# Transposing w3 by DMA instead of on TensorE, with its loads complete, a later start of the output product, and loads that wait for DMA transposes beside the first batch

## Chip, cores and metric

One core of a Trainium2 chip. The metric is the device time of one execution in microseconds (us). The engines carry the profile's names: PE is TensorE, PEld its weight loads, DVE VectorE, ACT ScalarE, POOL GpSimd, SP SyncE; a q behind a name (SPq, POOLq) marks a DMA that this engine issued. PSUM is the memory in which PE leaves its results, and from which ACT and DVE fetch them. Ratios in this document are the mean time of one kernel's runs over that of the other's runs of the same rounds, so they are not quite the ratio of the medians quoted beside them.

## The reference, cut to what matters

```python
# q, k, v: (4, 5824, 256); w1, w2: (256, 1024); w3: (1024, 1024); w_out: (1024, 256)
qn = q / (norm(q, axis=1) + 1e-6);  kn = k / (norm(k, axis=1) + 1e-6)
a = softmax(kn.transpose(0, 2, 1) @ qn / tau)     # 256 x 256 for each batch
x = (v @ a).reshape(4 * 5824, 256)
out = ((x @ w1) * (x @ w2)) @ w3 @ w_out
```

The kernel folds the small matrix of each batch into w1 and w2 ("folds", giving `Wf`), so a and b come directly from transposed v. It also multiplies w3 by w_out once (`W_sb`), so that the output product has 256 columns. For that product w3 must be transposed, and how this is done is what changes.

## The kernel before: the parts that matter

All work of one batch is issued in pairs: `emit_ab` computes 128 rows of a and of b for up to 512 tokens (a chunk), ACT casts a, DVE multiplies by b. Finished pairs are kept in `pend`; once `W_sb` is ready, `emit_out` multiplies them by it. Everything else hangs on an agenda: `at(t, cost, fn)` runs `fn` when the kernel's own clock (units of about a microsecond of TensorE work, zero at the start of a batch) reaches `t`.

```python
def pe_transpose(dst, src, tag, on_act):
    m = psum.tile([P, 8, P], BF16, tag=tag, ..., bufs={"ab": 4, "out": 3}[tag])
    for i, blk in enumerate(src):
        nc.tensor.transpose(m[:, i, :], blk, ident_b)
    if on_act: nc.scalar.copy(dst, m)
    else:      nc.vector.tensor_copy(dst, m)
...
def gate():                      # POOL waits for a recent product before it issues a load
    if last_ab[0] is not None:
        nc.gpsimd.tensor_copy(gate_t, last_ab[0][:1, :1])
...
for h in range(2):               # w3 in two halves, then w_out, then v's third piece
    js = slice(h * FT // 2, (h + 1) * FT // 2)
    nc.gpsimd.dma_start(out=w3_bf[:, js, :], in_=w3r[:, js, :])
nc.gpsimd.dma_start(out=wout_sb, ...)
load_piece("v", 0, 2)
...
def w3_transpose(jt):
    pe_transpose(w3T[jt // 2][:, jt % 2, :, :],
                 [w3_bf[:, jt, lt * P : (lt + 1) * P] for lt in range(FT)], "ab", jt % 2 == 0)

def w_unit(jt):                  # one of eight w products: W_sb[:, jt] = w3T . w_out
    m = psum.tile([P, 512], F32, tag="ab", ..., bufs=4)
    ...
# agenda of batch 0
for jt in range(FT):
    at((12.0 if jt < 4 else 15.0) + jt, 0.5, lambda jt=jt: w3_transpose(jt))
    at(24.0 + jt, 0.87, lambda jt=jt: w_unit(jt))
at(14.0, 0.0, lambda: transpose_piece(0, 2))       # v's third piece, by DMA
```

The a and b tiles, the w products, the folds and the transposes of w3 share four PSUM buffers (tag `ab`), used in turn.

## Time and profile before

| | before |
|---|---|
| time, median of the first three runs | 580.99 us (580.4 to 581.26) |
| span in the profile | 578.5 us |
| TensorE (PE) busy | 98% |
| VectorE (DVE), ScalarE (ACT) busy | 65%, 59% |
| PE transposes of w3 | 64, in 8 groups, from 52.99 us |

The prediction below shows the lines that carry this.

### The profile page before, as it was taken

The numbers are of one execution on the slowest core, as the hardware profiler recorded it, in microseconds if no ns is written. First come the engines' busy times: TensorE is split into PE (matmuls) and PEld (weight loads), VectorE is DVE, ScalarE is ACT, GpSimd is POOL, SyncE is SP. The second block draws the span as 40 slices with busy tenths as digits, with TensorE's granted clock in tenths as the row PEclk, the third lists the DMA queues.
The fourth block names the chain that finished last, engine by engine and source line by source line (L and its number), as shares of the span: only waits on it lengthen the run. The fifth ranks groups of instructions, "written<-read, shape, count | busy, mean of one in ns | idle before, by whom it ended". The sixth has DMA issues, their size and how long they took to land.

```text
span 578.5 us, 10224 instructions
## 1 busy us (share of the span) xinstructions
PE 565.4 (98%) x3826; PEld 360.8 (62%) x3834; DVE 376.8 (65%) x601; ACT 341.4 (59%) x628; POOL 64.1 (11%) x142
## 2 busy tenths in 40 slices
PE   8799999999999999999999999999999999999996
PEld 4665676766656566666666666666665656656664
DVE  0047545888877567788766667778876656565564
ACT  0046535777765576777765476767765554454453
POOL 5240021110000202001000112001100000000000
PEclk9999999999999999999999999999999999999999
DMA  8999989773543798555652699754563325311011
GB/s 164 211 206 199 172 152 208 162 167 78 120 100 109 132 233 167 111 113 122 129 126 74 147 199 177 166 110 87 146 133 87 83 77 146 83 41 71 37 73 56
DMA packets 66113, 74.85 MB, mean 129 GB/s; under 512 B 45840, under 2 KB 49808, under 8 KB 66064
## 3 DMA queue, kind: packets, MB, share of 16 engines
q0 software_dynamic: 15376, 39.46, 39.7%
q1 hardware_dynamic: 50544, 34.61, 20.0%
q8 instruction: 30, 0.49, 0.3%
q14 instruction: 19, 0.16, 0.1%
q10 hardware_dynamic: 144, 0.13, 0.1%
HBM read 78.91 MB, written 23.86 MB: 178 GB/s over the span
## 4 chain that ended last, share of the span: by engine, by line
PE 89%; DMA 6%; DVE 1%; ACT 1%; issue 1%; POOL 0%; ACTq 0%; POOLq 0%
PE o L452 27%; PE a L419 27%; PE b L419 26%; PE G L188 5%; DMA q<-in_q_dram 4%; PE fold L344 2%; PE w L570 1%; DMA v<-in_v_dram 1%; ACT as L425 1%; DVE abs L428 1%; POOL k L109 0%; DVE osb L473 0%; PE row L272 0%; PE ss L283 0%; ACT e L307 0%
## 5 line engine op out<-in xcount | busy, mean ns | idle before, releaser
L428 DVE TENSOR_TENSOR abs<-as,b 128x512 bf16<-128x512 bf16 x352 | 240.9, 687 | 147.5 <-ACT as L425 136.5
L425 ACT CAST as<-a 128x512 bf16<-128x512 f32 (+1 forms) x384 | 215.4, 562 | 172.6 <-DVE abs L428 83.7
L452 PE MATMUL o<-W_sb,abs 128*128 128x256 bf16 x1440 | 218.2, 273 | 0.5 <-ACT osb L472 0.4
L419 PEld LDWEIGHTS <-Wf 128*128 128x128 bf16 x1536 | 148.9, 98 | 98.2 <-issue 1.7
L419 PE MATMUL a<-vT,Wf 128*128 128x512 bf16 x704 | 209.6, 379 | 0.4
L419 PE MATMUL b<-vT,Wf 128*128 128x512 bf16 x704 | 209.5, 379 | 0.1
L452 PEld LDWEIGHTS <-abs 128*128 128x128 bf16 x1440 | 140.6, 98 | 86.3 <-issue 0.6
L197 DVE TENSOR_TENSOR acc<-acc,sq 128x1024 f32<-128x1024 f32 x66 | 80.4, 1218 | 0.1
L411 POOL COPY gate_t<-abs 1x1 bf16<-1x1 bf16 x39 | 10.3, 265 | 394.7 <-DVE abs L428 386.6
L188 PE MATMUL G<-k,q 128*128 128x256 bf16 x276 | 49.8, 273 | 0.0
L185 ACT ACTIVATE sq<-q 128x512 f32<-128x512 bf16 x66 | 41.8, 633 | 0.0
L185 ACT ACTIVATE sq<-k 128x512 f32<-128x512 bf16 x66 | 41.6, 630 | 0.0
L473 DVE COPY osb<-o 128x512 f32<-128x512 f32 x44 | 30.1, 685 | 0.4 <-PE o L452 0.4
L188 PEld LDWEIGHTS <-q 128*128 128x128 bf16 x276 | 27.0, 98 | 3.1
L472 ACT COPY osb<-o 128x512 f32<-128x512 f32 x44 | 25.7, 585 | 3.8 <-PE o L452 1.7
L274 ACT ACTIVATE kr<-row 128x256 f32<-128x256 f32 x4 | 1.5, 384 | 31.0 <-PE row L272 31.0
L109 POOL DMA_DIRECT2D q<-in_q_dram x28 | 15.0, 537 | 14.3 <-DMA k<-in_k_dram 5.7
L351 ACT ACTIVATE Wf<-fold,rs 128x512 bf16<-128x512 f32 x16 | 10.8, 687 | 8.9 <-PE fold L344 4.7
L344 PE MATMUL fold<-w,e 128*128 128x512 bf16 x61 | 16.0, 379 | 0.1
L109 POOL DMA_DIRECT2D v<-in_v_dram x25 | 13.5, 540 | 6.6 <-issue 4.9
L109 POOL DMA_DIRECT2D k<-in_k_dram x25 | 13.8, 550 | 3.4 <-DMA k<-in_k_dram 1.9
L353 DVE TENSOR_SCALAR Wf<-fold,rs 128x512 bf16<-128x512 f32 x16 | 11.8, 748 | 2.1 <-PE fold L344 1.8
(103 smaller groups left out, 197.3 us busy)
## 6 DMA issues: line engine op xcount, KB each, us to landing
out_dram<-osb SPq DMA_DIRECT2D x44, 512.0 KB, 3.0
k<-in_k_dram POOLq DMA_DIRECT2D x19, 512.0 KB, 8.9
v<-in_v_dram POOLq DMA_DIRECT2D x19, 512.0 KB, 5.2
q<-in_q_dram POOLq DMA_DIRECT2D x18, 512.0 KB, 5.9
w_wout<-in_moe_w_dram POOLq DMA_DIRECT2D x2, 1024.0 KB, 16.2
k<-in_k_dram POOLq DMA_DIRECT2D x4, 320.0 KB, 6.8
v<-in_v_dram POOLq DMA_DIRECT2D x4, 320.0 KB, 4.9
q<-in_q_dram POOLq DMA_DIRECT2D x4, 256.0 KB, 10.5
```

What stands on the lines that cost most here:

```text
L109: nc.gpsimd.dma_start(out=pieces[nm, n, pi][:, lo:hi, :], in_=qk_main[nm, n][0][:, pi * PIECE + lo : pi * PIECE + hi, :])
L185: nc.scalar.activation(out=dst[:, :, part, :], in_=src[:, o : o + 2, :], func=AF.Square)
L188: nc.tensor.matmul(G[:, ct, :], lhsT=qt[:, i, ct * P : (ct + 1) * P], rhs=kt[:, i, :], start=(pr == 0 and part == 0 and ct == 0), stop=(pr ...
L197: nc.vector.tensor_add(accs[n], accs[n], sqs[0])
L344: nc.tensor.matmul(st["fold", i], lhsT=st["e"][:, c2, c1 * P : (c1 + 1) * P], rhs=w12[:, c2, w, h * 512 : (h + 1) * 512], start=(c2 == 0), ...
L353: nc.vector.tensor_scalar_mul(dst, st["fold", i], st["rs"][:, c1 : c1 + 1])
L419: nc.tensor.matmul(t[:, :n], lhsT=Wf[b][:, ct, w, j * P : (j + 1) * P], rhs=rhs_of(b, c, ct), start=(ct == 0), stop=(ct == CT - 1),)
L425: nc.scalar.copy(a_sb[:, :n], tiles[0][:, :n])
L428: nc.vector.tensor_mul(ab, a_sb, tiles[1])
L452: nc.tensor.matmul(tl[s // 2][:, s % 2, :], lhsT=lhsT, rhs=W_sb[:, j, :], start=(j == 0 and s % 2 == 0), stop=(j == FT - 1 and (s % 2 == 1 ...
L472: nc.scalar.copy(o[:, 0:2, :], tl[0])
L473: nc.vector.tensor_copy(o[:, 2:4, :], tl[1])
```

## The change

The intent: take the transposes off PE, where time is scarce, and give them to the DMA queues. For that w3 is loaded whole, as the last of the early loads; four DMA transposes follow; the w products, and with them the output product, begin a little later; so more pairs must be kept, and the first 16 lie in free tiles of q. In batch 0 the first load after a DMA transpose of v waits ("hold") until that transpose has landed.

```diff
+    def hold(src):
+        nc.gpsimd.tensor_copy(gate_t, src)
...
+        if b == 0 and c < 2:
+            if j % 4 == 0:
+                held[0] = in_pool.tile([P, 4, 512], BF16, tag="q", ...)
+            ab = held[0][:, j % 4, :]
+        else:
+            ab = work.tile([P, 512], BF16, tag="ab_sb", ...)
...
+    def transpose_w3():
+        for h in range(FT // 2):
+            m = in_pool.tile([P, 2, FT, P], BF16, tag="k", ...)
+            nc.sync.dma_start_transpose(m, w3_bf[:, 2 * h : 2 * h + 2, :])
+            w3T.append(m)
...
-    for h in range(2):
-        js = slice(h * FT // 2, (h + 1) * FT // 2)
-        nc.gpsimd.dma_start(out=w3_bf[:, js, :], in_=w3r[:, js, :])
+    load_piece("v", 0, 2)
     nc.gpsimd.dma_start(out=wout_sb, ...)
-    load_piece("v", 0, 2)
+    nc.gpsimd.dma_start(out=w3_bf, in_=w3r)
...
+            at(15.0, 0.0, transpose_w3)
+            at(15.0, 0.0, lambda: transpose_piece(0, 2))
             for jt in range(FT):
-                at((12.0 if jt < 4 else 15.0) + jt, 0.5, lambda jt=jt: w3_transpose(jt))
-                at(24.0 + jt, 0.87, lambda jt=jt: w_unit(jt))
-            at(14.0, 0.0, lambda: transpose_piece(0, 2))
+                at(26.0 + 1.2 * jt, 0.87, lambda jt=jt: w_unit(jt))
# ... the loads of batch 0 get later times; scores of batch 1 (its products of k and q) from 58 (before 52) to 120 ...
+            if before is not None and b == 0:
+                at(t, 0.0, lambda w=before: hold(...))      # an element of the transposed v
```

More of the change, by code (lines that the diff above doesn't have):

```diff
@@ L406 @@
     last_ab = [None]
+    held = [None]
     def gate():
@@ L425, in emit_ab @@
         nc.scalar.copy(a_sb[:, :n], tiles[0][:, :n])
-        ab = work.tile([P, 512], BF16, tag="ab_sb", name=f"abs_{b}_{c}_{j}", bufs=8 * NDEF + 6)
+        if b == 0 and c < 2:
+            if j % 4 == 0:
+                held[0] = in_pool.tile([P, 4, 512], BF16, tag="q", name=f"abq_{c}_{j}", bufs=IN_BUFS["q"])
+            ab = held[0][:, j % 4, :]
+        else:
+            ab = work.tile([P, 512], BF16, tag="ab_sb", name=f"abs_{b}_{c}_{j}", bufs=8 * NDEF + 6)
         if n == 4 * P:
@@ L492 @@
     wout_sb = w3_wout[:, FT * F : FT * (F + D)].rearrange("p (l d) -> p l d", d=D)
-    w3T = {}
-    def new_w3T():
-        m = wf_pool.tile([P, 2, 2, FT, P], BF16, tag="Wf", name="w3T_wf")
-        for h in range(2):
-            w3T[h] = work.tile([P, 2, FT, P], BF16, tag="sq", name=f"w3T_{h}", bufs=2)
-            w3T[2 + h] = m[:, h]
+    w3T = []
+    def transpose_w3():
+        for h in range(FT // 2):
+            m = in_pool.tile([P, 2, FT, P], BF16, tag="k", name=f"w3T_{h}", bufs=IN_BUFS["k"])
+            nc.sync.dma_start_transpose(m, w3_bf[:, 2 * h : 2 * h + 2, :])
+            w3T.append(m)
     w3r = moe_w3.rearrange("(jh jl) l -> jl jh l", jl=P)
@@ L533 @@
     load_piece("v", 0, 1)
-    for h in range(2):
-        js = slice(h * FT // 2, (h + 1) * FT // 2)
-        nc.gpsimd.dma_start(out=w3_bf[:, js, :], in_=w3r[:, js, :])
+    load_piece("v", 0, 2)
     nc.gpsimd.dma_start(out=wout_sb, in_=moe_w_out.rearrange("(lh ll) c -> ll lh c", ll=P))
-    load_piece("v", 0, 2)
+    nc.gpsimd.dma_start(out=w3_bf, in_=w3r)
     squares("k", 4, whole)
@@ L556 @@
     soft0[4]()
-    new_w3T()
-    def w3_transpose(jt):
-        pe_transpose(
-            w3T[jt // 2][:, jt % 2, :, :], [w3_bf[:, jt, lt * P : (lt + 1) * P] for lt in range(FT)],
-            "ab", jt % 2 == 0,
-        )
     w_ready = [False]
@@ L591, in make_agenda @@
             at(8.0, 0.5, lambda: transpose_half_on_pe(0, 1, 1, False))
+            at(15.0, 0.0, transpose_w3)
+            at(15.0, 0.0, lambda: transpose_piece(0, 2))
             for jt in range(FT):
-                at((12.0 if jt < 4 else 15.0) + jt, 0.5, lambda jt=jt: w3_transpose(jt))
-                at(24.0 + jt, 0.87, lambda jt=jt: w_unit(jt))
-            at(14.0, 0.0, lambda: transpose_piece(0, 2))
-            loads = [("v", 0, 3, 14.0), ("v", 0, 4, 34.0), ("v", 0, 5, 54.0)]
-            loads += [("qk", 1, pi, t) for pi, t in enumerate([22.0, 30.0, 40.0, 52.0, 66.0, 80.0])]
@@ L598, in make_agenda @@
-            loads += [("v", 1, pi, t) for pi, t in enumerate([96.0, 108.0, 122.0])]
-            t0, t1 = 52.0, 120.0
-        else:
-            loads = [("v", b, pi, t) for pi, t in [(3, 1.0), (4, 20.0), (5, 34.0)]]
+                at(26.0 + 1.2 * jt, 0.87, lambda jt=jt: w_unit(jt))
+            moves = [("v", 0, 3, 29.0), ("qk", 1, 0, 38.0), ("qk", 1, 1, 43.0), ("v", 0, 4, 50.0), ("qk", 1, 2, 58.0)]
+            moves += [("qk", 1, 3, 63.0), ("v", 0, 5, 70.0), ("qk", 1, 4, 81.0), ("qk", 1, 5, 87.0)]
@@ L602, in make_agenda @@
+            moves += [("v", 1, 0, 96.0), ("v", 1, 1, 106.0), ("v", 1, 2, 116.0)]
+            t0, t1 = 58.0, 120.0
+        else:
+            moves = [("v", b, 3, 1.0), ("qk", n, 0, 4.0), ("qk", n, 1, 12.0), ("v", b, 4, 20.0), ("qk", n, 2, 27.0)]
+            moves += [("v", b, 5, 34.0), ("qk", n, 3, 44.0), ("qk", n, 4, 58.0), ("qk", n, 5, 72.0)]
+            moves += [("v", n, 0, 84.0), ("v", n, 1, 96.0), ("v", n, 2, 108.0)]
+            moves = [m for m in moves if m[1] < B]
             t0, t1 = 16.0, 104.0
-            if n < B:
-                loads += [("qk", n, pi, t) for pi, t in enumerate([4.0, 12.0, 27.0, 44.0, 58.0, 72.0])]
-                loads += [("v", n, pi, t) for pi, t in enumerate([84.0, 96.0, 108.0])]
@@ L606, in make_agenda @@
-        for nm, m, pi, t in loads:
+        before = (0, 2) if b == 0 else None
+        for nm, m, pi, t in moves:
+            if before is not None and b == 0:
+                at(t, 0.0, lambda w=before: hold(vTs[w[0]][1][:1, 0, :1] if w[1] == NP_ - 1 else vTs[w[0]][0][:1, w[1] * PIECE, 0, :1]))
+            at(t, 0.0, gate)
             if nm == "qk":
-                at(t, 0.0, gate)
                 at(t, 0.0, lambda m=m, pi=pi: load_qk(m, pi))
+                before = None
             else:
-                at(t, 0.0, gate)
@@ L612, in make_agenda @@
                 at(t, 0.0, lambda m=m, pi=pi: load_piece("v", m, pi))
-                at(t + 8.0, 0.0, lambda m=m, pi=pi: transpose_piece(m, pi))
+                at(t + (4.0 if b == 0 else 8.0), 0.0, lambda m=m, pi=pi: transpose_piece(m, pi))
+                before = (m, pi)
         if n == B:
```

## The prediction

> **What bounds the kernel now.** I read the page's busy shares first, then the chain of work that ended last, then the timeline of the stretch that the change touches (50 to 80 us), then where the batches meet (172 to 188 us), and last the DMA landings by stretch.
>
> ```profile
> PE 565.4 (98%) x3826; PEld 360.8 (62%) x3834; DVE 376.8 (65%) x601; ACT 341.4 (59%) x628; POOL 64.1 (11%) x142
> PE 89%; DMA 6%; DVE 1%; ACT 1%; issue 1%; POOL 0%; ACTq 0%; POOLq 0%
> ```
>
> PE is the bound: 98% busy, and 89% of the chain is PE. The 6% of DMA in the chain is the start (loads until about 37 us), which the change leaves alone: the same loads come in the same order up to the second piece of v. So time can only be won by taking work or idle gaps off PE, and can only be lost by new gaps on it. As "busy" is no proof of full speed, I also counted columns: matmuls in each 10 us, at 2.4 columns per ns, fill 9.4 to 10.9 us of each stretch from 40 us to 570 us. The only holes are 60 to 70 us (0.56 us) and the batch changes (about 0.5 us at 170, 300 and 440 us). A hidden reserve of ten microseconds does not exist.
>
> What the change touches is this, from the timeline of 28 to 80 us (columns: start, length, engine, line, operation, and in brackets the idle time before and who ended it):
>
> ```profile
> 52.12 0.59 PE L419 MATMUL a<-vT,Wf 128*128 128x512 bf16 x2
> 52.55 0.59 PE L419 MATMUL b<-vT,Wf 128*128 128x512 bf16 x2
> 52.99 0.61 PE L132 MATMUL tr_I-703_704<-ident_b,w_wout 128*128 128x128 bf16 x8
> 53.43 0.60 PE L419 MATMUL a<-vT,Wf 128*128 128x512 bf16 x2
> 53.63 1.01 ACT L134 COPY w3T<-tr_I-703_704 128x1024 bf16<-128x1024 bf16 x1 [0.29 <-PE tr_I-703_704 L132]
> ...
> 55.77 0.68 DVE L136 COPY w3T<-tr_I-724_725 128x1024 bf16<-128x1024 bf16 x1
> ...
> 56.51 0.43 PEld L132 LDWEIGHTS <-w_wout 128*128 128x128 bf16 x7 [0.29 <-issue]
> ...
> 62.46 0.43 PEld L132 LDWEIGHTS <-w_wout 128*128 128x128 bf16 x7 [0.41 <-issue]
> ...
> 65.38 1.03 PE L570 MATMUL w<-w_wout,w3T 128*128 128x256 bf16 x8
> 65.38 0.75 PEld L570 LDWEIGHTS <-w3T 128*128 128x128 bf16 x7 [0.41 <-issue]
> ```
>
> The reader is to see three things. A group of eight transposes starts at 52.99 and the next matmul starts at 53.43, so it takes 0.44 us of PE, 55 ns each, although one is listed with 219 ns (latency). Each group is copied out of PSUM by ACT (1.01 us) or DVE (0.68 us), between the casts and products of the a/b pairs. And in three places the weight load sat idle 0.29 to 0.41 us, called "issue": the next transpose or product waited for a PSUM buffer that such a copy still held.
>
> **What the Trainium skill says.** "TensorE: Matmul & The Clock Gate", section "Part 4: PE-mode transpose", gives about 275 ns for a 128x128 transpose in one kernel's context, with a copy out of PSUM after it. The trace agrees on the copy; as a cost in a pipelined group it measures 55 ns, and I use that: with 275 ns the gain would look like 17.6 us, which is wrong here. "Advanced Engine Details and Errata", section "X-Bar Transpose (TRN2)", says that transpose DMAs are as fast as regular ones. The trace agrees only where nothing else moves (512 KB):
>
> ```profile
> vT<-v SPq DMA_TRANSPOSE x1, 3.6
> ...
> vT<-v SPq DMA_TRANSPOSE x1, 9.3
> ```
>
> The first is from 150 to 162 us, the second from 80 to 100 us with q, k and v loads beside it; the last number is us from issue to landing. "DMA: Bandwidth & Descriptors", section "Rules for kernel authors", says that a transpose next to ordinary DMAs needs nothing. So the new waits are not for correctness; they keep transposes from being stretched.
>
> **The change part by part.**
> Removed from PE: 64 transposes of w3, 8 groups x 0.445 us = 3.56 us. Waits around them: from 52.99 to 65.38 us are 12.39 us, in which nine a/b pairs run. A pair is 0.86 us (52.12 to 52.99 less rounding), so 7.74 us; the remaining 4.65 us are transposes (3.56) and about 1.1 us of gaps. From 40.42 (first pair) to 52.99 the same count leaves no gap, and from 65.38 to the first output product at 75.60 none either. So the whole stretch offers 4.6 us.
> Removed from ACT and DVE: 4 x 1.01 and 4 x 0.68 us. Worth nothing beyond those gaps, as neither bounds this stretch (at 0.58 and 0.69 us per pair against PE's 0.86).
> Added: four DMA transposes of w3, 512 KB each, on SP's queue, ahead of the transpose of v's third piece. They start when w3 is in. In the kernel before the last of the early loads was v's third piece, and the first DMA transpose, which waits for it, starts at 58.54:
>
> ```profile
> 58.54 6.61 SPq L155 DMA_TRANSPOSE vT<-v  x2
> ```
>
> Now w3 is last, the bytes are the same, so I take 58.5 for w3. With the loads held back, each takes 3.6 to 3.9 us to land; wholly one after the other they land at 62.4, 66.3, 70.2, 74.1 and v's piece at 78.0; overlapped, with an issue of about 1.6 us each, by about 70.
> Needed: the changed order on PE puts the first w product after 28 pairs, two folds and three groups of v transposes: 40.42 + 28 x 0.86 + 2 x 0.43 + 3 x 0.445 = 66.7 us; then w1 at 68.4, w2 and w3 at 70.2, w4 and w5 at 72.8, w6 and w7 at 75.4, and chunk 4, the first that reads v's third piece, at 77.1. Each tile serves two w products (needed 66.7, 70.2, 72.8, 75.4). Even the serial landing meets all four and misses chunk 4 by 0.9 us; the overlapped one has 4 us or more to spare. I choose no stall.
> Moved: the output product begins about 1.5 us later (37.3 us of PE work after the first pair, before 33.8), with 33 products waiting in place of 25. That is the same PE work in another order, and there are 54 buffers (38 and the 16 in q's free tiles), so no wait. Loads of the second batch come later, but the kernel before shows no PE wait for any load after 40 us, and the scores also start later (58 in place of 52 on the kernel's own clock).
>
> **Given back.** The chain that prepares batch 1 stays at fixed times while batch 0 gets 3.4 us shorter, so its eight folds slide into the last, small chunk. I count from the first fold to batch 1's first product in the changed order: PE 8 folds x 0.43 + 8 small pairs x 0.33 + outputs 1.5 = 7.6 us. DVE in it: one product 0.69, four copies of folds x 0.75, one output copy 0.69, eight pairs x (0.29 + 0.22) = 8.5 us. In the kernel before the same section is 11.5 us of PE against 10.5 of DVE. There the small chunk already ran DVE-bound in part: its eight pairs took 182.72 to 187.23 = 4.5 us for 4.1 us of PE work. So about 0.9 us more DVE than PE, softened by the two pairs that PE can run ahead, worsened by ACT's copies in between: I put 0.8 us. The scores are packed into 62 in place of 68 units beside a DVE near full, for which I put 0.2 us.
> Sum: -4.6 + 0.8 + 0.2 = -3.6 us: 580.99 - 3.6 = 577.4.
>
> **Rivals.**
> First, w3 arrives late, or its transposes run slowly, and PE waits at the w products: a wait in place of the work removed. For it: the first two transposes before ran beside a load and one took 6.9 us; w3 is now one 2 MB load instead of two. Against: the holds leave the DMA queues empty from 58.5 to about 70 us. A delay of x beyond about 4 us costs x - 4; at 6.9 us each in series the fourth lands at 86 against 75.4 needed, about 11 us lost and 588. I give a stall of over 2 us 12%.
> Second, DVE becomes the bound where batches meet and takes back 2 us or more: 579. For it: the count above. Against: only one boundary moves this way; in batches 1 to 3 nothing is changed but the absolute time. 15%.
> Third, the holds free loads and transposes of contention and that gives more than I say. Against: no PE wait for them exists after 40 us, so it is hidden anyway: 576.4 at best, if the boundary costs nothing too.
>
> **Range and chances.** The ceiling of the gain, 4.6 us, is fixed by counts: 576.4, or 575.8 with scatter (three runs before span 0.9 us). The lower end is 575.6. Upwards the two rivals: 580.2 leaves the kernel unchanged nearly. Over 2% faster needs 11.6 us, more than twice the work removed: 1%. Over 2% slower needs a stall of 15 us: 2%. Within 2%: 97%.
>
> **What would show it.** Right: no transposes of w3 on PE; the gap from the last a/b pair before 66.7 to the first w product nil; the four DMA transposes issued at about 58.5 and landed by 66 to 74; first output product at about 78 to 79; batch 1's first product near 183.5 in place of 187.2, with DVE busy and PE gaps near it; the rest the same shifted. Wrong: PE waiting at a w product or at chunk 4 for a DMA, waits of the scores for q or k of batch 1, or PE gaps of over 2 us between 170 and 185 us.

## More of the kernel before

To compare the two kernels later, four points in time of PE are used: the first a/b pair, the first output product, the row sum that starts the preparation of batch 1, and the first pair of batch 1. In the timeline before (start and length in us, engine, line, operation):

```profile
40.42 0.60 PE L419 MATMUL a<-vT,Wf 128*128 128x512 bf16 x2
...
75.81 1.04 PE L452 MATMUL o<-W_sb,abs 128*128 128x256 bf16 x8
...
164.80 0.60 PE L272 MATMUL row<-acc,ones_pp 128*128 128x256 f32 x2
...
187.23 0.59 PE L419 MATMUL a<-vT,Wf 128*128 128x512 bf16 x2
```

## The result and the profile after

The changed kernel takes 576.26 us (median of 4 runs, 576.16 to 577.95), before 581.12 us in the same rounds. The ratio is 0.9925 (95% interval 0.9905 to 0.9946), that is 4.4 us less (581.12 x 0.0075). Executions over 1.5% slower than the fastest of the same kernel are left out of the means.

The page's busy shares and the chain of the changed kernel:

```profile
PE 561.9 (98%) x3770; PEld 356.8 (62%) x3770; DVE 374.7 (65%) x597; ACT 338.6 (59%) x624; POOL 65.9 (11%) x147
PE 90%; DMA 6%; ACT 1%; issue 1%; DVE 1%; POOL 1%; ACTq 0%; POOLq 0%
```

PE is still the bound, with 3.5 us less to do. The timeline of the changed kernel, the stretch that the change touches:

```profile
40.49 0.59 PE L424 MATMUL a<-vT,Wf 128*128 128x512 bf16 x2
...
58.48 8.20 SPq L510 DMA_TRANSPOSE w3T<-w_wout  x4
...
66.58 0.59 PE L424 MATMUL b<-vT,Wf 128*128 128x512 bf16 x2
...
67.01 1.04 PE L571 MATMUL w<-w_wout,w3T 128*128 128x256 bf16 x8
...
72.08 0.18 POOL L416 COPY gate_t<-vT 1x1 bf16<-1x1 bf16 x1 [35.06 <-DMA vT<-v]
...
77.45 0.59 PE L424 MATMUL a<-vT,Wf 128*128 128x512 bf16 x2
...
78.31 1.04 PE L463 MATMUL o<-W_sb,abq 128*128 128x256 bf16 x8
```

The four DMA transposes are issued from 58.48 on. The first w product follows the pair before it at 67.01 (66.58 + 0.43) with no gap. POOL's hold ends at 72.08: by then v's third piece is transposed, 5 us before chunk 4 reads it at 77.45. Then, later in the same timeline:

```profile
164.29 0.60 PE L272 MATMUL row<-acc,ones_pp 128*128 128x256 f32 x2
...
183.38 0.59 PE L424 MATMUL a<-vT,Wf 128*128 128x512 bf16 x2
```

From these points the gain can be followed:

| PE at | before | after | what it says |
|---|---|---|---|
| first pair | 40.42 | 40.49 | same start |
| first output product | 75.81 | 78.31 | from the first pair 35.39 and 37.82 us; after has run 8 pairs more (33, not 25), 8 x 0.863 = 6.90 us, so it is 35.39 + 6.90 - 37.82 = 4.5 us ahead |
| row sum | 164.80 | 164.29 | see below |
| first pair of batch 1 | 187.23 | 183.38 | 3.85 us ahead |
| first pair of batch 2, of batch 3 | 320.75, 454.11 | 316.91, 450.27 | still 3.84 us ahead |

For the stretches between I take PE's own work: the columns of all matmuls in the program's order (a few records are missing from the traces) at the pace of undisturbed pairs with their outputs, 3072 columns in 1.300 us. The few f32 and one-column sums, the same in both kernels, come to 1536 columns in this count; that is an allowance, so the differences between kernels are firmer than each excess by itself. From the first output product to the row sum both kernels are 0.2 us above it. From the row sum to batch 1 the kernel before is 1.20 us above (22.43 against 21.23), the changed one 1.76 (19.09 against 17.33). So 4.5 us are won at the transposes, about 0.6 given back at the first batch change, and nothing moves after that.

### The profile page after: what moved, and what is told of

Its sections match the earlier page's. It is cut to its first block, busy times and chain, and to the rows that moved or that the text cites. A ratio compares the mean times of both kernels' runs of the same rounds, so it can differ in the third digit from the quotient of the medians.

```text
span 574.4 us, 10119 instructions
## 1 busy us (share of the span) xinstructions
PE 561.9 (98%) x3770; PEld 356.8 (62%) x3770; DVE 374.7 (65%) x597; ACT 338.6 (59%) x624; POOL 65.9 (11%) x147
## 4 chain that ended last, share of the span: by engine, by line
PE 90%; DMA 6%; ACT 1%; issue 1%; DVE 1%; POOL 1%; ACTq 0%; POOLq 0%
PE o L463 27%; PE a L424 27%; PE b L424 27%; PE G L188 5%; DMA q<-in_q_dram 4%; PE fold L344 2%; PE w L571 1%; DMA v<-in_v_dram 1%; ACT as L430 1%; POOL k L109 0%; DVE abs L439 0%; DVE osb L484 0%; PE row L272 0%; POOL q L109 0%; PE ss L283 0%
## 5 line engine op out<-in xcount | busy, mean ns | idle before, releaser
L439 DVE TENSOR_TENSOR abs<-as,b 128x512 bf16<-128x512 bf16 x336 | 229.9, 687 | 140.1 <-ACT as L430 128.6
L463 PE MATMUL o<-W_sb,abs 128*128 128x256 bf16 x1376 | 209.7, 273 | 0.5 <-ACT osb L483 0.4
L463 PEld LDWEIGHTS <-abs 128*128 128x128 bf16 x1376 | 134.5, 98 | 82.0 <-issue 0.6
L109 POOL DMA_DIRECT2D q<-in_q_dram x28 | 15.1, 539 | 14.2 <-DMA k<-in_k_dram 5.4
L351 ACT ACTIVATE Wf<-fold,rs 128x512 bf16<-128x512 f32 x16 | 10.9, 687 | 7.2 <-PE fold L344 4.9
L439 DVE TENSOR_TENSOR abq<-as,b 128x512 bf16<-128x512 bf16 x16 | 10.9, 686 | 3.9 <-ACT as L430 3.4
## 6 DMA issues: line engine op xcount, KB each, us to landing
q<-in_q_dram POOLq DMA_DIRECT2D x4, 256.0 KB, 10.5
```

The costliest lines, as they stand in the source:

```text
L109: nc.gpsimd.dma_start(out=pieces[nm, n, pi][:, lo:hi, :], in_=qk_main[nm, n][0][:, pi * PIECE + lo : pi * PIECE + hi, :])
L351: nc.scalar.activation(out=dst, in_=st["fold", i], func=AF.Copy, scale=st["rs"][:, c1 : c1 + 1])
L439: nc.vector.tensor_mul(ab, a_sb, tiles[1])
L463: nc.tensor.matmul(tl[s // 2][:, s % 2, :], lhsT=lhsT, rhs=W_sb[:, j, :], start=(j == 0 and s % 2 == 0), stop=(j == FT - 1 and (s % 2 == 1 ...
```

## The experiments

Twelve runs. Where a run is compared with the changed kernel, the point to look at is "batch 0", the time from the first pair to the first pair of batch 1 in the profile: 142.89 us in the changed kernel (183.38 - 40.49). It leaves out the start, which differs by up to a microsecond between runs with the early loads.

### The changed kernel again (two runs)

No edit, as a yardstick beside the others.

> The changed kernel itself, unedited, as the yardstick for the runs beside it. Both theories: 4.1 to 4.9 us below the kernel before (ratio 0.9915 to 0.993), first w product at 67.0 us, first output product at 78.3 us, batch 1's first product at 183.4 us in the profile.

> The changed kernel again, as the yardstick for the two runs beside it: ratio 0.992 to 0.993, from the first product of batch 0 to that of batch 1 142.9 us in the profile, the next two batches 133.5 and 133.4 us.

Measured: 576.09 us, ratio 0.9924 (0.9912 to 0.9937), and 576.59 us, ratio 0.9923 (0.9911 to 0.9936); batch 0 takes 142.88 and 142.86 us. So the gain is 4.4 us three times over, and batch 0 repeats to 0.03 us in these profiles.

### PE transposes put back, without copies

```diff
+    def idle_transpose(jt, copied):
+        m = psum.tile([P, 8, P], BF16, tag="ab", name=f"idle_{jt}", bufs=4)
+        for i in range(8):
+            nc.tensor.transpose(m[:, i, :], w12[:, i % 2, i // 4, jt * P : (jt + 1) * P], ident_b)
...
+                at((12.0 if jt < 4 else 15.0) + jt, 0.0, lambda jt=jt: idle_transpose(jt, False))
                 at(26.0 + 1.2 * jt, 0.87, lambda jt=jt: w_unit(jt))
```

> The changed kernel with 64 TensorE transposes put back (of w1, which is in by then), in eight groups at the old places, without any copy out of PSUM; the results are not used. Theory (PE's issue time is what was removed): 8 x 0.445 = 3.56 us longer than the changed kernel, 579.9 or so, first w product at 70.5 us. Rival A (the transposes on PE were hidden, the gain comes from the DMA side: order of loads, holds, later output product): within 0.5 us of the changed kernel. Rival B (the copies on ACT and DVE were the cost): also within 0.5 us, and only the next run is slower.

Measured: 580.34 us, ratio to before 0.9992 (0.9978 to 1.0006), against 0.9924 of the changed kernel beside it: 0.0068 x 580.5 = 3.9 us longer. Batch 0 takes 146.46 us, 3.58 us longer (its start was also 0.95 us later, in the early loads, which the edit does not touch). The timeline of this run:

```profile
53.49 0.59 PE L424 MATMUL b<-vT,Wf 128*128 128x512 bf16 x2
53.92 0.61 PE L569 MATMUL idle<-ident_b,w 128*128 128x128 bf16 x8
54.37 0.59 PE L424 MATMUL a<-vT,Wf 128*128 128x512 bf16 x2
```

Each group takes 0.45 us from its start to the next matmul, and eight of them are the 3.58 us. Rival A (the transposes were hidden) and rival B (only the copies cost) both fall.

### The same with the copies out of PSUM

```diff
+        if copied:
+            d = work.tile([P, 2, FT, P], BF16, tag="sq", name=f"idled_{jt}", bufs=2)[:, 0]
+            (nc.scalar.copy if jt % 2 == 0 else nc.vector.tensor_copy)(d, m)
...
+                at((12.0 if jt < 4 else 15.0) + jt, 0.0, lambda jt=jt: idle_transpose(jt, True))
```

> As pe_only, and each group is also copied out of PSUM, by ACT and DVE in turn, as in the kernel before. Theory: 4.5 us longer than the changed kernel (3.56 for PE, 0.9 to 1.1 for the gaps in which the next matmul waits for a PSUM buffer), 580.8 or so, with gaps of 0.3 to 0.4 us beside the transposes again; that is the kernel before again less the give-back at the batch change. Rival A: within 0.5 us of the changed kernel. Rival B: 4.5 us, all of it here and none in pe_only.

Measured: 581.22 us, ratio 1.0013 (1.0001 to 1.0026); batch 0 takes 147.92 us, 5.04 us longer than in the changed kernel and 1.46 us longer than without the copies (by the ratios 1.2 us). The timeline of this run shows where:

```profile
53.69 1.01 ACT L572 COPY idled<-idle 128x1024 bf16<-128x1024 bf16 x1 [0.29 <-PE idle L569]
...
54.60 0.59 ACT L430 CAST as<-a 128x512 bf16<-128x512 f32 x1
...
55.22 0.69 DVE L439 TENSOR_TENSOR abq<-as,b 128x512 bf16<-128x512 bf16 x1 [1.10 <-ACT as L430]
...
55.46 0.10 PEld L569 LDWEIGHTS <-w 128*128 128x128 bf16 x1
...
55.96 0.43 PEld L569 LDWEIGHTS <-w 128*128 128x128 bf16 x7 [0.41 <-issue]
...
58.94 3.12 PEld L424 LDWEIGHTS <-Wf 128*128 128x128 bf16 x15 [0.41 <-issue]
```

One weight is loaded, then the next waits 0.41 us. The profile names no releaser ("issue"), but the times and the order of the four buffers do: the group at 55.96 takes the buffer of the pair's b tile four tiles earlier, and DVE's product, which reads that tile, ends at 55.91 (55.22 + 0.69). This product had waited 1.10 us for the cast on ACT, and the cast had stood behind ACT's copy of 1.01 us. The wait at 58.94 follows a product that ends at 58.88 in the same way. So ACT and DVE, though far from busy, cost PE: a copy on ACT delays the cast, the cast delays the product, and the product empties b's buffer late. The kernel before shows the same at 55.91, 62.46 and 65.38 (products end at 55.85, 62.41 and 65.33); only the wait that ends at 56.51 was for a buffer that a copy itself still held (it ends at 56.45). The effect was expected at 0.9 to 1.1 us; it is 1.46 here. In the kernel before, where 4.5 - 3.56 leaves 0.9, the groups stood a little differently between the pairs; that this is the reason for the difference was not tested.

### The output product at its old time

```diff
-                at(26.0 + 1.2 * jt, 0.87, lambda jt=jt: w_unit(jt))
+                at(24.0 + jt, 0.87, lambda jt=jt: w_unit(jt))
```

> The changed kernel with the eight w products where they stood before (units 24 to 31 in place of 26 to 34.4), so the output product begins earlier again. Theory: its later start is no part of the gain: the first w product is due at 65 us, the first transposed tile of w3 lands at 62.6 us and the others 2 us apart, so no wait; within 0.3 us of the changed kernel. Rival (the later start is needed, PE would wait for the transposes): 1 us or more longer, with PE waiting for w3T.

Measured: 576.64 us, ratio 0.9935 (0.992 to 0.9951), whose interval overlaps that of the changed kernel; batch 0 takes 142.94 us. No PE wait for w3T. The later start of the output product is no part of the gain; it is a margin for the DMA transposes.

### The output product earlier still

```diff
-                at(26.0 + 1.2 * jt, 0.87, lambda jt=jt: w_unit(jt))
+                at(20.0 + jt, 0.87, lambda jt=jt: w_unit(jt))
```

> As w24, at units 20 to 27: the first w product is due at about 61 us, before the first tile lands (62.6), and two products to each tile. Theory: PE now waits, 1.5 to 3 us in all for the DMA transposes of w3, and the kernel is that much longer than the changed one. Rival (the transposes land much earlier than the queue shows, or other work fills in): within 0.5 us.

Measured: 578.66 us, ratio 0.9975 (0.9951 to 0.9998); batch 0 takes 144.83 us, 1.95 us longer than in the changed kernel. (By the ratios it is 3.0 us, because one of the four runs took 581.42 us; the profile is of the fastest, 577.9.) The weight loads of this run:

```profile
62.32 0.77 PEld L571 LDWEIGHTS <-w3T 128*128 128x128 bf16 x8 [1.92 <-DMA w3T<-w_wout]
...
67.90 0.77 PEld L571 LDWEIGHTS <-w3T 128*128 128x128 bf16 x8 [0.46 <-DMA w3T<-w_wout]
```

This is the wait of the first rival, made on purpose. It also dates the transposes: the first tile is there at 62.3 us, the third (first read by the product at 67.90) at 67.8. The changed kernel's own trace has the four landing at 62.3, 64.3, 67.0 and 70.4 us, wanted at 67.0, 70.5, 73.1 and 75.7. So the change has 4.7 to 6.1 us in hand.

### No holds

```diff
-            if before is not None and b == 0:
+            if False:
```

> The changed kernel without the loads' waits for DMA transposes in batch 0. Theory: the holds are hidden from the end: within 0.5 us of the changed kernel, while transposes of 512 KB beside loads take 7 to 11 us to land again in batch 0. Rival (contention was part of the gain): 1 us or more longer, with PE waits for transposed v or for w3T.

Measured: 576.39 us, ratio 0.9928 (0.9914 to 0.9941); batch 0 takes 142.86 us. The holds are hidden, as expected. The other half of the expectation was a miss: the one 512 KB transpose that met a load (issued at 98.9 us, q's load at 100.6) was stretched only to 5.3 us (4.4 with holds). With the loads at these times few meet a transpose. What a collision can cost showed only in the last run below.

### The old order of the loads

```diff
-    load_piece("v", 0, 2)
+    for h in range(2):
+        js = slice(h * FT // 2, (h + 1) * FT // 2)
+        nc.gpsimd.dma_start(out=w3_bf[:, js, :], in_=w3r[:, js, :])
     nc.gpsimd.dma_start(out=wout_sb, ...)
-    nc.gpsimd.dma_start(out=w3_bf, in_=w3r)
+    load_piece("v", 0, 2)
```

> The changed kernel with w3 loaded in two halves ahead of w_out and of v's third piece, as before. Theory: w3 is in by about 53 us in place of 58.5, its first transposes run beside loads, all land before 66.7 us, so PE sees nothing: within 0.3 us of the changed kernel. Rival (complete loads ahead of the transposes are needed): transposes stretched to 7 us and more, PE waits at w products or at the first pair of chunk 4, 1 us or more longer.

Measured: 576.45 us, ratio 0.9929 (0.9913 to 0.9944); batch 0 takes 142.89 us. The first two transposes were issued at 48.4 and 50.0 us, beside the remaining loads, and the DMA landings from 49 to 53 us show what that did to them:

```profile
w3T<-w_wout SPq DMA_TRANSPOSE x2, 15.1
```

15.1 us in place of 4.1 (both are medians of the two). The queue of SP was blocked by the second until 62.8; the last was issued at 65.1 and took 6.1 us, so the expectation that all would land by 66.7 was wrong. But it landed at 71.2, ahead of its product at 75.7, and PE saw nothing. "Loads complete" is a margin too, not a part of the gain.

### Batch 1's softmax and folds earlier

```diff
-            t0, t1 = 58.0, 120.0
+            t0, t1 = 58.0, 116.5
```

> The changed kernel with batch 1's scores ending, and its norms, softmax and folds starting, 3.5 units earlier in batch 0 (116.5 in place of 120), so that they stand to the end of batch 0 as in the kernel before. Theory (the folds that slid into the small last chunk made DVE the bound there): 0.5 to 0.6 us shorter than the changed kernel; from the first row sum to batch 1's first product only 1.2 us above PE's own work in place of 1.76. Rival (the packed scores beside a full DVE cost as much): no gain or a loss, since the scores are packed tighter still, 58.5 units in place of 62.

Measured: 575.97 us, ratio 0.992 (0.9907 to 0.9932), beside 0.9924; batch 0 takes 142.79 us, 0.09 us shorter. That is no clear gain and misses the expected 0.5 to 0.6 us, yet not because the folds stayed costly. From the first fold to batch 1 this run is 0.39 us above PE's own work, as the kernel before was (0.38), where the changed kernel is 0.91 above. But ahead of it a wait has grown:

```profile
168.26 0.38 PE L463 MATMUL o<-W_sb,abs 128*128 128x256 bf16 x2 [0.85 <-ACT osb L483]
```

The exponentials on ACT now fall just ahead of the copy that empties an output tile, and PE waits 0.85 us for it; in the changed kernel it waits 0.39 us at that place. The wait was moved, not removed.

### Exponentials in mid-chunk, one fold to a pair

```diff
         ts = [t1 + 1.0, t1 + 3.5, t1 + 4.0, t1 + 8.0, t1 + 12.0] + [t1 + 13.0 + 0.9 * i for i in range(8)]
+        if b == 0:
+            ts = [t1 + 1.0, t1 + 3.5, t1 + 4.0, t1 + 7.5, t1 + 10.5] + [t1 + 11.5 + 1.73 * i for i in range(8)]
-            t0, t1 = 58.0, 120.0
+            t0, t1 = 54.0, 111.0
```

> The changed kernel with batch 1's softmax chain moved so that its exponentials fall in the middle of a chunk (away from the output copy on ACT, on which PE waited 0.85 us in soft_early) and its folds one to a pair, all done before the small last chunk. Theory (give-back at the batch change is DVE and ACT queueing on folds and exponentials, nothing of the transposes): batch 0 takes 141.6 us in place of 142.9 (the 1.7 us above PE's own work from the first row sum to batch 1 fall to 0.5 or less), the time 1.0 to 1.3 us shorter than the changed kernel; the rest as it is. Rival (scores packed into 57 units in place of 62 make DVE the bound earlier): batch 0 takes 142.9 us or more, with the loss now before the row sum.

Measured: 582.67 us (577.78 to 584.35), ratio 1.0015 (0.9986 to 1.0043): slower than the changed kernel and scattered. Batch 0 takes 150.16 us. The batch change itself did improve: from the row sum to batch 1 27.31 us, 0.88 above PE's own 26.43, in place of 1.76. But the scores, moved earlier, now reach their loads:

```profile
140.58 0.58 PE L188 MATMUL G<-k,q 128*128 128x256 bf16 x2 [5.35 <-DMA k<-in_k_dram]
```

So neither theory as written: not DVE, but k. And the wait costs a second time (us; busy and instructions of PE, PEld, DVE, ACT, POOL; granted clock of PE; DMA share; GB/s):

```profile
137.90:140.50 2.60, 0.00 (x0) 0.00 (x0) 0.00 (x0) 0.00 (x0) 0.00 (x0) 0.50 1.03 242
140.60:144.60 4.00, 4.00 (x16) 2.16 (x16) 0.34 (x1) 1.71 (x3) 0.00 (x0) 0.50 0.84 178
```

PE is granted half its clock from 137.85 us, 2.6 us after it fell idle, to 144.68, that is for 4.1 us after it has work again. The profiled run is one of the slow ones of this kernel (583.74).

### The same at all batch changes

```diff
-        ts = [t1 + 1.0, t1 + 3.5, t1 + 4.0, t1 + 8.0, t1 + 12.0] + [t1 + 13.0 + 0.9 * i for i in range(8)]
+        ts = [t1 + 1.0, t1 + 3.5, t1 + 4.0, t1 + 7.5, t1 + 10.5] + [t1 + 11.5 + 1.73 * i for i in range(8)]
-            t0, t1 = 58.0, 120.0
+            t0, t1 = 54.0, 111.0
-            t0, t1 = 16.0, 104.0
+            t0, t1 = 14.0, 102.0
```

> The same spreading at all three batch changes, the version meant to beat both kernels. Theory: as soft_mid, and batches 1 and 2 each 0.4 to 0.8 us shorter (133.0 in place of 133.5), so 2 to 2.5 us shorter than the changed kernel in all, about 574, ratio 0.988 to 0.989 to the kernel before. Rival: no gain in batches 1 and 2, where chunk 11 already held no folds.

Measured: 583.92 us, with two runs at 576.5 and four from 583.2 to 584.9; ratio 1.0028 (0.9987 to 1.007). The profile fell on a run of 576.52: there the scores waited 1.03 us for k, the batch change was again 0.88 us above PE's own work, and batches 1 and 2 took 133.41 and 133.60 us. The four profiles of the kernels without these edits have 133.52 or 133.53 for batch 1 and 133.36 to 133.98 for batch 2, so the expected 0.4 to 0.8 us in each are not there. So even in an undisturbed run it is no faster than the changed kernel.

### The loads moved ahead as well, without holds

The edits of spread_all, `if False:` in place of the holds, and:

```diff
-            moves = [("v", 0, 3, 29.0), ("qk", 1, 0, 38.0), ("qk", 1, 1, 43.0), ("v", 0, 4, 50.0), ("qk", 1, 2, 58.0)]
-            moves += [("qk", 1, 3, 63.0), ("v", 0, 5, 70.0), ("qk", 1, 4, 81.0), ("qk", 1, 5, 87.0)]
+            moves = [("v", 0, 3, 29.0), ("qk", 1, 0, 34.0), ("qk", 1, 1, 39.0), ("qk", 1, 2, 47.0), ("v", 0, 4, 55.0)]
+            moves += [("qk", 1, 3, 60.0), ("qk", 1, 4, 69.0), ("qk", 1, 5, 78.0), ("v", 0, 5, 86.0)]
```

> spread_all with the loads of batch 1's q and k moved ahead in batch 0 (the last two at units 69 and 78 in place of 81 and 87, v's last piece after them at 86) and without the holds. Theory (soft_mid and spread_all lost time only because the scores, moved earlier, reached their loads): the scores no longer wait for q or k, batch 0 takes 142.0 us (0.88 above PE's own work at the change, as both showed, in place of 1.76), no run near 583, and the time is 0.9 to 1.5 us below the changed kernel, ratio 0.9895 to 0.991 to the kernel before. Rival (the tighter scores themselves are at fault, or transposes and loads without holds collide): times scatter by several us again, with PE waits in batch 0.

Measured: 580.32 us (577.52 to 586.9), ratio 0.9984 (0.9962 to 1.0006). Batch 0 takes 147.13 us. The rival's words came true. v's fourth piece was being transposed when q and k were loaded; the DMA landings from 76 to 80 us of this run:

```profile
q<-in_q_dram POOLq DMA_DIRECT2D x1, 512.0 KB, 13.8
k<-in_k_dram POOLq DMA_DIRECT2D x1, 512.0 KB, 20.3
vT<-v SPq DMA_TRANSPOSE x1, 22.8
```

and of the changed kernel, where the load is held until the transpose has landed, from 76 to 84 us:

```profile
q<-in_q_dram POOLq DMA_DIRECT2D x1, 512.0 KB, 5.0
k<-in_k_dram POOLq DMA_DIRECT2D x1, 512.0 KB, 7.6
vT<-v SPq DMA_TRANSPOSE x1, 3.7
```

Beside each other they took about three to six times as long, and the first score product waited 3.28 us for k. The two edits are not separated here: without holds but with the loads at their later times (no_hold) the same transpose took 3.6 us, so leaving out the holds is not enough to cause it. What follows the wait costs again. Busy time in stretches of this run (columns as in soft_mid):

```profile
95.00:98.00 3.00, 0.00 (x0) 0.00 (x0) 0.00 (x0) 0.00 (x0) 0.00 (x0) 1.00 1.11 187
98.00:100.00 2.00, 1.97 (x8) 0.97 (x8) 0.03 (x1) 0.96 (x2) 0.00 (x0) 0.64 1.02 263
100.00:102.00 2.00, 2.00 (x12) 1.40 (x11) 0.65 (x1) 0.68 (x2) 0.70 (x2) 0.51 1.11 295
102.00:104.00 2.00, 2.00 (x16) 1.42 (x15) 0.66 (x1) 1.11 (x2) 0.00 (x0) 1.00 0.98 272
```

After 3.28 us with nothing to do PE is granted 0.50 of its clock from 98.55 to 101.97 us, which the windows average to 0.64 and 0.51. The Trainium skill says so on "TensorE: Matmul & The Clock Gate", section "Why this matters for your kernels": no idle gaps above about 3 us, or the clock drops. The two traces agree: waits of 3.28 and 5.35 us were followed by half the clock, waits of PE of 1.03 us (spread_all) and 1.43 us (w20) were not. It fits the scatter of the last three kernels too. Their runs are of two kinds: every one of 579.9 us or more has a mean granted clock of 0.989 to 0.997, every faster one 0.998 to 1.000. That a late k stands behind each slow run is not shown, as only one run of each kernel has a profile; and the mean alone proves little, as two ordinary runs of the changed kernel (576.57 and 577.95 us) have 0.996.

No version of mine beats the changed kernel.

## Why the prediction was right, point by point

- The ceiling, 4.6 us off PE: measured 4.5 us by the first output product. Its main term, 8 x 0.445 us of issue, is shown by itself: 3.58 us in pe_only. Its second, about 1.1 us of gaps, is real too: 0.9 in the change, 1.46 us when put back in pe_copies. Its reason was half right: of four waits before (the working counts three; the one at 55.91 is missing) one was for a copy's own buffer, three were for b's buffer behind a product that ACT's copy had delayed.
- w3 complete at 58.5, transposes in time, no stall: transposes issued at 58.48, no wait for them in the profile, 4.7 to 6.1 us in hand. The landing of v's third piece, by 72.1 us, lies between the two estimates (70 and 78).
- The output product and the loads begin later at no cost: w24 and no_hold show both to be free, old_order the same for the order of loads. The output product began 2.4 us later after the first pair, not "about 1.5": the sums 37.3 and 33.8 do not give 1.5, and 37.82 and 35.39 were measured.
- Given back where batches meet: 0.8 us was put down, 0.56 measured (1.76 less 1.20). The sign and place were right, the reason was not, so that the size came near was luck: the working had DVE with 8.5 us of work in 7.6 us, but in the profile DVE is busy 6.46 us of the 8.50 us of that section (76%). The listed durations of short DVE instructions overlap (in the trace they start 0.20 us apart at 0.29 us each), so their sum overstates the work. I read the loss as a queue of PE, ACT and DVE behind four PSUM buffers and not as a full engine; no run isolates it, and for stretches of about a microsecond DVE is full there (179.00 to 180.00: 1.00 us busy). Moving the folds out removed it (soft_early, 0.39 from the first fold on), and brought another wait.
- Packed scores: 0.2 us was put down; both kernels are 0.2 us above PE's work in that stretch, so it was nothing.
- The sum said -3.6 us and 577.4; the timed ratio says -4.4 us. With the two small terms at their measured size the sum is -4.5 + 0.6 = -3.9, the 3.85 us that the profile shows at batch 1; its whole span is 4.1 us shorter. The remaining 0.3 us lie within the interval of the ratio, and in the profile after the last store has landed (1.3 us to the end before, 1.0 after), which the change does not touch; they stay open.
- The rivals: late transposes (did not happen; w20 shows that wait to be real when asked for), DVE at the boundary taking 2 us or more (0.56), gain from relieved DMA queues (none; pe_only gives 3.6 of 4.5 us back with the holds in place).
- Two misreadings that the sum does not use: the first output product before starts at 75.81, not 75.60 (that is its first weight load); and the columns, counted again from the records, fill 9.1 to 10.5 us of each 10 us, not 9.4 to 10.9, with two gaps between 55 and 57 us besides the holes that were named.

## What to carry to other kernels

On an engine that bounds the kernel, price an operation by the time from its start to the next one's start, not by its listed duration, and add what the handling of its results delays: here a copy on ACT held up the cast, the product and so PE's next buffer. When work moves to an idle resource, compute when it lands and when it is read; the difference is the margin to defend, and here it was about 5 us (4.7 at the least). A DMA transpose and loads in flight together can slow each other several times, which costs nothing until somebody waits; waits of 3.28 and 5.35 us then cost TensorE a second time in clock.

## What the Trainium skill lacked or had wrong

- "TensorE: Matmul & The Clock Gate", "Part 4: PE-mode transpose": 275 or 390 ns for a 128x128 transpose. In groups of eight, back to back, each costs PE 55 ns (0.445 us for eight; 64 put back cost 3.58 us), though each is listed with 219 ns.
- "Advanced Engine Details and Errata", "X-Bar Transpose (TRN2)": transposes as fast as regular DMAs. Alone yes (512 KB in 3.7 us, a load of as much 5.2 us; four in a row 3.9 to 6.0 us each, all landed 11.9 us after the first was issued). It gives no figure for a transpose beside loads: 15.1 us (old_order) and 22.8 us (loads_first), and the loads suffer too: k 20.3 in place of 7.6 us.
- "DMA: Bandwidth & Descriptors", "Rules for kernel authors": a transpose next to ordinary DMAs needs nothing. Both experiments without holds (no_hold, loads_first) were correct, which agrees; the row says nothing of time, for which it mattered in loads_first (22.8 us) and not in no_hold (3.6 and 5.3 us).
